# Moving the query and key transposes of an attention plus MoE kernel from TensorE to DMA, from the second batch on

## The chip, the cores and the metric

The kernel runs on one core of one Trainium2 chip. The metric is the device time of one execution in microseconds (us). A ratio is the mean time of one kernel's fast runs over that of the other's fast runs of the same rounds, so it is not quite the ratio of the medians that are quoted; its interval is a 95% one. Differences under 2% count as "the same".

## The reference, cut to what matters

```python
# q, k, v: (4, 8, 768, 64) float32; heads 0, 2, 6 "retrieval", the others "streaming"
scores = q @ k.T / 8            # per batch and head
# retrieval: causal mask; streaming: causal and (first 4 keys, or the last 64)
a = softmax(scores); attn = a @ v
x = attn, heads side by side    # (3072, 512)
p = domain_probs / sum          # (3072, 4)
out = sum over e of p[:, e] * (relu(x @ w1[e]) @ w2[e])   # 4 experts, 512 -> 1024 -> 512
```

## The kernel before

The 3072 rows are cut into eight groups of 384 (two per batch). The MoE (the layer of four experts) of group g and the attention of group g+1 are woven into one stream of work on TensorE (PE): an attention step is put in whenever the attention is behind its share of the MoE time. PE works in program order, so the weaving is fixed when the program is built.

```python
for g in range(G):
    nxt = g + 1
    if nxt < G: att_steps = attention(nxt // NCH, nxt % NCH)
    if g + 2 < G:
        load_qk(...); load_v(...)                 # of group g + 2, GpSimd queue
    begin = 0.55 * UNIT if g == 0 else 0.0        # UNIT: one expert, 10.4 us
    end = 2.6 * UNIT if g == 0 else 0.93 * E * UNIT
    att_ns = 6400.0 if nxt % NCH == 0 else 10200.0
    for ns in moe_group(g):
        spent += ns
        while done < (spent - begin) / (end - begin) * att_ns:
            step = next(att_steps, None)          # ... one attention step
```

A score needs queries and keys with the 64 head dimensions on the partitions, so both are transposed, two heads at a time, by a matmul with the identity, and copied by VectorE (DVE) out of PSUM, the memory that PE writes its results to. `bank()` is one of four PSUM banks that transposes, scores and the first MoE layer take in turn.

```python
def transposes(hp):
    for x, is_k in ((xk, 1), (xq, 0)):
        ps = bank()
        for j in range(3):
            nc.tensor.matmul(out=ps[:, j*P:(j+1)*P], lhsT=x[:, j, 2*hp:2*hp+2, :], rhs=ident, ...)
        # queries: one copy of 128 x 384 to qT[hp]
        # keys: two copies of 64 x 384, each head to its half of a tile whose other half is zero
        ...
```

The softmax here doesn't subtract the row's maximum and nothing guards it: scores larger than these inputs give would overflow.

Of the kernel before, what the change touches and what calls it, by code (L numbers as in the profile page):

```python
# [17 lines left out]
def kernel(  # L18
# [69 lines left out]
    kz = []  # L88
    vR = []
    vS = []  # L90
    for i in range(2):
        kz.append(
            [
                pers.tile([P, NT, P] if not RETR[h] else [P, S], FP16, name=f"kz{i}_{h}")
                for h in range(H)
            ]
        )
        vR.append(pers.tile([P, S // P, len(RH), P], FP16, name=f"vR{i}"))
        vS.append(pers.tile([P, NT, len(SH), P], FP16, name=f"vS{i}"))
# [15 lines left out]
    def v_cols(h):  # L115
        u = h % 2
        return slice(u * D, (u + 1) * D)

# [9 lines left out]
    k16 = {}  # L128
# [7 lines left out]
    def alloc_qk(b, c):  # L136
        q16[b, c] = att.tile([P, 3, H, D], FP16, name="q16", bufs=2)
        k16[b, c] = att.tile([P, 3, H, D], FP16, name="k16", bufs=2)

    def load_qk(b, c):  # L140
        alloc_qk(b, c)
        for x, x16 in ((q, q16[b, c]), (k, k16[b, c])):
            for j in range(3):
                s0 = c * CH + j * P
                gp.dma_start(  # L145
                    out=x16[:, j, :, :],
                    in_=x[b, :, s0 : s0 + P, :].rearrange("h p d -> p h d"),
                )

    def load_v(b, c, heads):  # L150
        for h in heads:
            t = v_tile(b, h)
            if RETR[h]:
                gp.dma_start(  # L154
                    out=t[:, 3 * c : 3 * c + 3, v_cols(h)], in_=rows_of(v, b, h, c)
                )
            else:
                gp.dma_start(  # L158
                    out=t[R0:P, TC * c : TC * (c + 1), v_cols(h)],
                    in_=tiles_of(v, b, h, c),  # L160
                )

    def sink_rows(op, b, h, c):
        t = v_tile(b, h)[:, :, v_cols(h)]
        op(
            out=t[0:NS, TC * c : TC * (c + 1), :],
            in_=t[R0 : R0 + NS, 0:1, :].to_broadcast([NS, TC, D]),
        )
# [30 lines left out]
    def zero_keys(eng, i, h, c):  # L199
        if RETR[h]:  # L200
            fill(eng, kz[i][h][:, c * CH : (c + 1) * CH], 0.0)
        else:
            t = kz[i][h].rearrange("p t x -> p (t x)")
            fill(eng, t[:, c * TC * P : (c + 1) * TC * P], 0.0)
# [38 lines left out]
    for h in range(H):  # L243
        zero_keys(nc.vector, 0, h, 0)
# [47 lines left out]
    load_qk(0, 1)  # L292
# [15 lines left out]
    def attention(b, c):  # L308
        g = b * NCH + c
        i = b % 2  # L310
        qT = {}
# [3 lines left out]
        def transposes(hp):  # L315
            xk, xq, ident = (
                (k32, q32, ident32) if first else (k16[b, c], q16[b, c], ident16)
            )
            qT[hp] = att.tile([P, CH], FP16, name=f"qT{hp}", bufs=2)
            for x, is_k in ((xk, 1), (xq, 0)):  # L320
                ps = bank()
                for j in range(3):
                    o = ps[:, j * P : (j + 1) * P]
                    i_ = x[:, j, 2 * hp : 2 * hp + 2, :]
                    if first:
                        nc.tensor.transpose(o, i_, ident)
                    else:
                        nc.tensor.matmul(out=o, lhsT=i_, rhs=ident, start=True, stop=True)  # L328
                if not is_k:
                    nc.vector.tensor_copy(out=qT[hp], in_=ps[:, 0:CH])  # L330
                    yield 3 * mm_ns(P)
                    continue
                for u in range(2):
                    h = 2 * hp + u
                    r = slice(u * D, (u + 1) * D)
                    if RETR[h]:
                        nc.vector.tensor_copy(  # L337
                            out=kz[i][h][r, c * CH : (c + 1) * CH], in_=ps[r, 0:CH]
                        )
                        continue  # L340
                    nc.vector.tensor_copy(  # L341
                        out=kz[i][h][r, TC * c : TC * (c + 1), R0:P],
                        in_=ps[r, 0:CH].rearrange("r (t x) -> r t x", x=TK),
                    )

                    if b == 0 and c == 0:
                        sink_k[h] = pers.tile([P, NS], FP16, name=f"sk{h}")
                        nc.vector.tensor_copy(out=sink_k[h][r, :], in_=ps[r, 0:NS])
                    if c == 0:
                        nt = TC if b == 0 else NT  # L350
                        nc.vector.tensor_copy(
                            out=kz[i][h][r, 0:nt, 0:NS],
                            in_=ps[r, 0:NS]
                            .rearrange("r (o x) -> r o x", o=1)
                            .to_broadcast([D, nt, NS]),
                        )
                    elif b == 0:
                        nc.scalar.copy(
                            out=kz[i][h][r, TC:NT, 0:NS],
                            in_=sink_k[h][r, :]  # L360
                            .rearrange("r (o x) -> r o x", o=1)
                            .to_broadcast([D, NT - TC, NS]),
                        )
                yield 3 * mm_ns(P)
# [38 lines left out]
        def scores(h):  # L403
            hp = h // 2
            es_of[h] = []
            for cols, parts, masks in score_tiles(h):
                ps = bank()
                ns = 0
                for n, (t, o, q0, nq) in enumerate(parts):
                    lhsT = kz[i][h][:, t * P : (t + 1) * P] if RETR[h] else kz[i][h][:, t, :]  # L410
                    nc.tensor.matmul(  # L411
                        out=ps[:, o : o + nq],
                        lhsT=lhsT,
                        rhs=qT[hp][:, q0 : q0 + nq],
                        start=(n == 0 or not first),
                        stop=not first,
                        skip_group_check=first,
                    )
                    ns += mm_ns(nq)
# [85 lines left out]
        yield from transposes(0)  # L505
        yield from transposes(1)
        if first:

            def sinks(*heads):
                for h in heads:  # L510
                    sink_rows(nc.vector.tensor_copy, b, h, c)
# [13 lines left out]
        else:  # L525
            for h in SH:
                sink_rows(nc.sync.dma_start, b, h, c)
            yield from scores(0)
            for h in range(1, H):
                if h % 2 == 0 and h // 2 + 1 < HP:  # L530
# [78 lines left out]
    for h in range(H):  # L609
        zero_keys(nc.vector, 0, h, 1)  # L610
    for h in range(H):
        zero_keys(gp, 1, h, 0)
        zero_keys(gp, 1, h, 1)
# [17 lines left out]
    for g in range(G):  # L631
# [4 lines left out]
        if g + 2 < G:  # L636
            load_qk((g + 2) // NCH, (g + 2) % NCH)
            load_v((g + 2) // NCH, (g + 2) % NCH, range(H))
# [3 lines left out]
        pos = nxt % NCH  # L642
        att_ns = 6400.0 if pos == 0 else 10200.0
        spent = 0.0
        done = 0.0
        for ns in moe_group(g):
            spent += ns
            while done < (spent - begin) / (end - begin) * att_ns:
# [41 lines left out]
```

## Time and profile before

| | before |
|---|---|
| time, median | 428.46 us |
| span of the profiled run | 426.0 us |
| PE busy | 96% |
| ScalarE (ACT) busy | 59% |
| DVE busy | 47% |
| MoE group 0, with the loading of all weights | 58.1 us |
| groups 1, 3, 5 (attention with 384 keys or fewer inside): "short" | 48.0 us each |
| groups 2, 4, 6 (attention with up to 768 keys inside): "long" | 52.3 us each |
| group 7, no attention inside | 41.5 us |

The group lengths are read from the timeline of PE: a group runs from its first first-layer matmul to that of the next group. They repeat to 0.05 us between groups of a kind; the whole time scatters by 1 to 2 us. The lines themselves stand in the prediction.

### The profile page before, as it was taken

The numbers are of one execution on the slowest core, as the hardware profiler recorded it, in microseconds if no ns is written. First come the engines' busy times: TensorE is split into PE (matmuls) and PEld (weight loads), VectorE is DVE, ScalarE is ACT, GpSimd is POOL, SyncE is SP. The second block draws the span as 40 slices with busy tenths as digits, with TensorE's granted clock in tenths as the row PEclk, the third lists the DMA queues.
The fourth block names the chain that finished last, engine by engine and source line by source line (L and its number), as shares of the span: only waits on it lengthen the run. The fifth ranks groups of instructions, "written<-read, shape, count | busy, mean of one in ns | idle before, by whom it ended". The sixth has DMA issues, their size and how long they took to land.

```text
span 426.0 us, 6784 instructions
## 1 busy us (share of the span) xinstructions
PE 408.4 (96%) x2608; PEld 231.8 (54%) x2608; DVE 198.5 (47%) x433; ACT 251.7 (59%) x544; POOL 101.4 (24%) x155
## 2 busy tenths in 40 slices
PE   6689899999999999999999999999999999999996
PEld 3445554555555555555555555555555555555552
DVE  7657442555525454355545444355544445432222
ACT  5856784356755756556773559646674577653331
POOL 8746915902700045000810009000000000000000
PEclk9989999999999999999999999999999999999999
DMA  9999999932901049100932009120001000020001
GB/s 171 151 184 147 198 209 142 168 24 16 98 33 43 2 31 81 51 26 2 92 21 76 2 0 103 10 76 1 2 0 62 16 0 2 1 75 0 2 0 74
DMA packets 89228, 25.45 MB, mean 60 GB/s; under 512 B 79981, under 2 KB 84077, under 8 KB 89197
## 3 DMA queue, kind: packets, MB, share of 16 engines
q0 software_dynamic: 75552, 17.05, 43.8%
q1 hardware_dynamic: 12044, 7.59, 6.0%
q10 hardware_dynamic: 1600, 0.39, 0.5%
q8 instruction: 20, 0.33, 0.3%
q14 instruction: 12, 0.09, 0.1%
HBM read 35.70 MB, written 6.29 MB: 99 GB/s over the span
## 4 chain that ended last, share of the span: by engine, by line
PE 81%; ACT 8%; DMA 6%; POOL 2%; issue 2%; DVE 1%; POOLq 0%; ACTq 0%
PE pO L572 38%; PE pA L551 32%; PE pV L457 5%; PE pA L411 4%; DMA w2sb<-in_moe_w_dram 3%; ACT hs L564 3%; DMA vR<-in_v_dram 2%; PE pA L328 2%; ACT rc L476 2%; ACT es L429 1%; ACT rc L486 1%; POOL vS L158 1%; POOL vR L154 1%; DVE kz L341 0%; DVE kz L337 0%
## 5 line engine op out<-in xcount | busy, mean ns | idle before, releaser
L551 PE MATMUL pA<-xT,w1sb 128*128 128x384 f16 x1024 | 192.0, 328 | 3.1 <-ACT hs L564 1.7
L572 PE MATMUL pO<-w2sb,hs 128*128 128x512 f16 x768 | 185.1, 379 | 0.0
L564 ACT ACTIVATE hs<-pA 128x384 f16<-128x384 f32 x256 | 121.5, 495 | 89.3 <-PE pA L551 87.7
L551 PEld LDWEIGHTS <-w1sb 128*128 128x128 f16 x1024 | 96.0, 98 | 60.4 <-issue 6.3
L572 PEld LDWEIGHTS <-hs 128*128 128x128 f16 x768 | 72.0, 98 | 69.0 <-ACT hs L564 2.6
L429 ACT ACTIVATE es<-pA 128x256 f16<-128x256 f32 (+3 forms) x152 | 72.1, 486 | 47.0 <-PE pA L411 43.5
L588 DVE SCALAR_TENSOR_TENSOR acc<-pO,p_sb,acc 128x512 f32<-128x512 f32 x72 | 53.9, 749 | 76.9 <-PE pO L572 76.4
L145 POOL DMA_DIRECT2D q<-in_q_dram x21 | 18.6, 895 | 137.1 <-PE pA L411 81.3
L411 PE MATMUL pA<-qT,kz 128*128 128x160 f16 (+5 forms) x300 | 47.6, 244 | 1.6 <-ACT es L429 1.0
L433 DVE TENSOR_TENSOR es<-es,mS 128x384 f16<-128x384 f16 (+1 forms) x70 | 22.2, 317 | 57.7 <-ACT es L429 56.9
L476 ACT ACTIVATE rc<-pV,eps 64x384 f32<-64x384 f32 x60 | 34.6, 576 | 24.2 <-PE pV L457 23.3
L481 DVE TENSOR_TENSOR xT<-pV,rc 64x384 f16<-64x384 f32 x60 | 33.2, 553 | 22.6 <-PE pA L551 11.2
L411 PEld LDWEIGHTS <-kz 128*128 128x128 f16 x300 | 27.3, 98 | 23.0 <-issue 2.3
L486 ACT ACTIVATE rc<-rc 64x384 f32<-64x384 f32 x58 | 30.2, 521 | 1.9
L158 POOL DMA_DIRECT2D vS<-in_v_dram x40 | 28.2, 710 | 9.9 <-DMA w2sb<-in_moe_w_dram 4.3
L433 DVE TENSOR_TENSOR es<-es,mC 128x256 f16<-128x256 f16 (+1 forms) x42 | 10.7, 256 | 36.9 <-ACT es L429 36.9
L584 DVE TENSOR_SCALAR acc<-pO,p_sb 128x512 f32<-128x512 f32 x24 | 18.0, 750 | 17.6 <-PE pO L572 17.5
L341 DVE CAST kz<-pA 64x384 f16<-64x384 f32 x40 | 22.3, 557 | 2.6 <-PE pA L328 1.1
L457 PE MATMUL pV<-es,vR 128*128 128x384 f16 (+2 forms) x120 | 21.7, 278 | 0.8 <-ACT es L429 0.7
L154 POOL DMA_DIRECT2D vR<-in_v_dram x24 | 18.5, 770 | 10.5 <-DMA w2sb<-in_moe_w_dram 5.4
L145 POOL DMA_DIRECT2D k<-in_k_dram x21 | 18.6, 910 | 4.5 <-DMA w2sb<-in_moe_w_dram 4.2
L457 PEld LDWEIGHTS <-vS 128*128 128x128 f16 x180 | 13.9, 98 | 10.4 <-issue 4.7
(60 smaller groups left out, 155.4 us busy)
## 6 DMA issues: line engine op xcount, KB each, us to landing
out_dram<-acc SPq DMA_DIRECT2D x24, 256.0 KB, 2.0
w1sb<-in_moe_w_dram POOLq DMA_DIRECT2D x4, 1024.0 KB, 15.4
w2sb<-in_moe_w_dram POOLq DMA_DIRECT2D x4, 1024.0 KB, 16.4
q<-in_q_dram POOLq DMA_DIRECT2D x21, 128.0 KB, 4.0
k<-in_k_dram POOLq DMA_DIRECT2D x21, 128.0 KB, 5.4
vS<-in_v_dram POOLq DMA_DIRECT2D x40, 48.0 KB, 3.3
vR<-in_v_dram POOLq DMA_DIRECT2D x24, 48.0 KB, 4.0
k<-in_k_dram SPq DMA_DIRECT2D x8, 96.0 KB, 4.0
```

What stands on the lines that cost most here:

```text
L145: gp.dma_start(out=x16[:, j, :, :], in_=x[b, :, s0 : s0 + P, :].rearrange("h p d -> p h d"),)
L411: nc.tensor.matmul(out=ps[:, o : o + nq], lhsT=lhsT, rhs=qT[hp][:, q0 : q0 + nq], start=(n == 0 or not first), stop=not first, skip_group_ ...
L429: nc.scalar.activation(out=es[:, 0:cols], in_=ps[:, 0:cols], func=AF.Exp, scale=SC)
L433: nc.vector.tensor_tensor(out=es[:, o0:o1], in0=es[:, o0:o1], in1=m[:, mo : mo + o1 - o0], op=ALU.mult,)
L457: nc.tensor.matmul(out=ps[:, q0 : q0 + nq], lhsT=v_tile(b, h)[:, t, :], rhs=es[:, o : o + nq], start=(n == 0), stop=(n == len(work) - 1), ...
L476: nc.scalar.activation(out=rc[r, :], in_=ps[o, 0:CH], func=AF.Ln, bias=eps[o, :])
L481: nc.vector.tensor_tensor(out=xT[g][r, hp, :], in0=ps[r, 0:CH], in1=rc[r, :], op=ALU.mult)
L486: nc.scalar.activation(out=rc[r, :], in_=rc[r, :], func=AF.Exp, scale=-1.0)
L551: nc.tensor.matmul(out=pss[ft][:, 0:CH], lhsT=w1sb[:, e * DMP + ct, ft * P : (ft + 1) * P], rhs=xT[g][:, ct, :], start=(ct == 0), stop=(ct ...
L564: nc.scalar.activation(out=hs[:, ft, :], in_=ps[:, 0:CH], func=AF.Relu)
L572: nc.tensor.matmul(out=ps_o, lhsT=hs[:, ft, j * P : (j + 1) * P], rhs=w2sb[:, e * FTP + ft, :], start=(ft == 0), stop=(ft == FTP - 1),)
L588: nc.vector.scalar_tensor_tensor(out=acc[nt], in0=ps_o, scalar=p_ap, in1=acc[nt], op0=ALU.mult, op1=ALU.add,)
```

## The change

The intent: give the 144 transposes of groups 2 to 7 to the DMA engines, so that PE and DVE lose them. Keys are loaded already spread over zeroed 128-column blocks, and five transposing DMAs per group (SBUF to SBUF) turn 41 blocks of 128x128. The pacing of the attention is set anew as well. The core of the diff:

```diff
+    def dma_transposes(b, c):
+        nc.sync.dma_start(out=kSr[c][0:NS, ...], in_=first.to_broadcast(...))   # sink rows
+        alloc_qT(b, c)
+        for j in range(3):
+            nc.sync.dma_start(out=qTs[b, c][:, :, j * P : (j + 1) * P],
+                in_=q16[b, c][:, j, :, :].rearrange("p h d -> p (h d)"), transpose=True)
+        for x, xr in ((kR, kRr), (kS, kSr)):        # 9 and 20 blocks
+            nc.sync.dma_start(out=x[i][:, c, ...], in_=xr[c]..., transpose=True)
...
-        yield from transposes(0)
-        yield from transposes(1)
+        by_dma = b > 0
+        if not by_dma:
+            alloc_qT(b, c)
+            yield from transposes(0)
+            yield from transposes(1)
...
-    for h in range(H):
-        zero_keys(nc.vector, 0, h, 1)
+    zero(nc.vector, kR[0][:, 1, :, :, :])
+    zero(nc.vector, kS[0][:, 1, :, :, :])
...
-            load_qk((g + 2) // NCH, (g + 2) % NCH)
+            load_k(b2, c2)
+            load_q(b2, c2)
...
-        att_ns = 6400.0 if pos == 0 else 10200.0
+        att_ns = 4500.0 if nxt % NCH == 0 else 7700.0
+        if nxt < NCH:
+            att_ns += 8 * 3 * mm_ns(P)
...
+            if to_transpose and spent > 0.5 * E * UNIT:
+                dma_transposes(*divmod(g + 2, NCH))
```

More of the change, by code (lines that the diff above doesn't have):

```diff
@@ L87 @@
     w2sb = pers.tile([P, E * FTP, DM], FP16, name="w2sb")
-    kz = []
+    NR, NSH = len(RH), len(SH)
+    kR = []
+    kS = []
     vR = []
@@ L91 @@
     for i in range(2):
-        kz.append(
-            [
-                pers.tile([P, NT, P] if not RETR[h] else [P, S], FP16, name=f"kz{i}_{h}")
-                for h in range(H)
-            ]
-        )
+        kR.append(pers.tile([P, NCH, 3, NR, P], FP16, name=f"kR{i}"))
+        kS.append(pers.tile([P, NCH, TC, NSH, P], FP16, name=f"kS{i}"))
         vR.append(pers.tile([P, S // P, len(RH), P], FP16, name=f"vR{i}"))
@@ L112, with own, key_tile @@
     p_sb = pers.tile([P, NTILE, E], FP32, name="p_sb")
-    def v_cols(h):
+    kRr = [pers.tile([P, 3, NR, P], FP16, name=f"kRr{c}") for c in range(NCH)]
+    kSr = [pers.tile([P, TC, NSH, P], FP16, name=f"kSr{c}") for c in range(NCH)]
+    def own(h):
         u = h % 2
         return slice(u * D, (u + 1) * D)
+    def key_tile(b, h, t):
+        i = b % 2
+        if RETR[h]:
+            return kR[i][:, t // 3, t % 3, RH.index(h), :]
+        return kS[i][:, t // TC, t % TC, SH.index(h), :]
     def v_tile(b, h):
@@ L127 @@
     q16 = {}
-    k16 = {}
     def rows_of(x, b, h, c):
@@ L134, in tiles_of, with load_by_rows, load_q, load_k @@
         return x[b, h, c * CH : (c + 1) * CH, :].rearrange("(t r) d -> r t d", r=TK)
-    def alloc_qk(b, c):
-        q16[b, c] = att.tile([P, 3, H, D], FP16, name="q16", bufs=2)
-        k16[b, c] = att.tile([P, 3, H, D], FP16, name="k16", bufs=2)
-    def load_qk(b, c):
-        alloc_qk(b, c)
-        for x, x16 in ((q, q16[b, c]), (k, k16[b, c])):
-            for j in range(3):
-                s0 = c * CH + j * P
+    def load_by_rows(x, x16, b, c):
+        for j in range(3):
+            s0 = c * CH + j * P
+            gp.dma_start(
+                out=x16[:, j, :, :],
+                in_=x[b, :, s0 : s0 + P, :].rearrange("h p d -> p h d"),
+            )
+    def load_q(b, c):
+        q16[b, c] = att.tile([P, 3, H, D], FP16, name="q16", bufs=2)
+        load_by_rows(q, q16[b, c], b, c)
+    def load_k(b, c):
+        for h in range(H):
+            if RETR[h]:
                 gp.dma_start(
-                    out=x16[:, j, :, :],
-                    in_=x[b, :, s0 : s0 + P, :].rearrange("h p d -> p h d"),
-                )
+                    out=kRr[c][:, :, RH.index(h), own(h)], in_=rows_of(k, b, h, c)
+                )
+            else:
+                gp.dma_start(
+                    out=kSr[c][R0:P, :, SH.index(h), own(h)], in_=tiles_of(k, b, h, c)
+                )
+    qTs = {}
+    def alloc_qT(b, c):
+        qTs[b, c] = att.tile([P, HP, CH], FP16, name="qT", bufs=2)
+    def dma_transposes(b, c):
+        i = b % 2
+        first = kSr[0][R0 : R0 + NS, 0:1, :, :].rearrange("p t s x -> p t (s x)")
+        nc.sync.dma_start(
+            out=kSr[c][0:NS, :, :, :].rearrange("p t s x -> p t (s x)"),
+            in_=first.to_broadcast([NS, TC, NSH * P]),
+        )
+        alloc_qT(b, c)
+        for j in range(3):
+            nc.sync.dma_start(
+                out=qTs[b, c][:, :, j * P : (j + 1) * P],
+                in_=q16[b, c][:, j, :, :].rearrange("p h d -> p (h d)"),
+                transpose=True,
+            )
+        for x, xr in ((kR, kRr), (kS, kSr)):
+            nc.sync.dma_start(
+                out=x[i][:, c, :, :, :].rearrange("p t s x -> p (t s) x"),
+                in_=xr[c].rearrange("p t s x -> p (t s x)"),
+                transpose=True,
+            )
     def load_v(b, c, heads):
@@ L154, in load_v @@
                 gp.dma_start(
-                    out=t[:, 3 * c : 3 * c + 3, v_cols(h)], in_=rows_of(v, b, h, c)
+                    out=t[:, 3 * c : 3 * c + 3, own(h)], in_=rows_of(v, b, h, c)
                 )
@@ L158, in load_v, with sink_row, sink_rows @@
                 gp.dma_start(
-                    out=t[R0:P, TC * c : TC * (c + 1), v_cols(h)],
+                    out=t[R0:P, TC * c : TC * (c + 1), own(h)],
                     in_=tiles_of(v, b, h, c),
                 )
-    def sink_rows(op, b, h, c):
-        t = v_tile(b, h)[:, :, v_cols(h)]
-        op(
+    def sink_row(b, h, c):
+        t = v_tile(b, h)[:, :, own(h)]
+        nc.vector.tensor_copy(
             out=t[0:NS, TC * c : TC * (c + 1), :],
             in_=t[R0 : R0 + NS, 0:1, :].to_broadcast([NS, TC, D]),
+        )
+    def sink_rows(b, c):
+        x = vS[b % 2].rearrange("p t s x -> p t (s x)")
+        nc.sync.dma_start(
+            out=x[0:NS, TC * c : TC * (c + 1), :],
+            in_=x[R0 : R0 + NS, 0:1, :].to_broadcast([NS, TC, NSH * P]),
         )
@@ L197, in fill, with zero @@
             eng.memset(ap, value)
-    def zero_keys(eng, i, h, c):
-        if RETR[h]:
-            fill(eng, kz[i][h][:, c * CH : (c + 1) * CH], 0.0)
-        else:
-            t = kz[i][h].rearrange("p t x -> p (t x)")
-            fill(eng, t[:, c * TC * P : (c + 1) * TC * P], 0.0)
+    def zero(eng, t):
+        fill(eng, t.rearrange("p t s x -> p (t s x)"), 0.0)
     def one_values(eng, i, c):
@@ L242 @@
     load_v(0, 0, [0, 1, 2, 3])
-    for h in range(H):
-        zero_keys(nc.vector, 0, h, 0)
+    zero(nc.vector, kR[0][:, 0, :, :, :])
+    zero(nc.vector, kS[0][:, 0, :, :, :])
     nc.vector.tensor_copy(out=ident16, in_=ident32)
@@ L291 @@
     load_w2(0)
-    load_qk(0, 1)
+    load_q(0, 1)
+    k16 = att.tile([P, 3, H, D], FP16, name="k16", bufs=1)
+    load_by_rows(k, k16, 0, 1)
     load_w1(1, 0, F)
@@ L310, in attention @@
         i = b % 2
-        qT = {}
         first = g == 0
@@ L316, in transposes @@
             xk, xq, ident = (
-                (k32, q32, ident32) if first else (k16[b, c], q16[b, c], ident16)
+                (k32, q32, ident32) if first else (k16, q16[b, c], ident16)
             )
-            qT[hp] = att.tile([P, CH], FP16, name=f"qT{hp}", bufs=2)
             for x, is_k in ((xk, 1), (xq, 0)):
@@ L329, in transposes @@
                 if not is_k:
-                    nc.vector.tensor_copy(out=qT[hp], in_=ps[:, 0:CH])
+                    nc.vector.tensor_copy(out=qTs[b, c][:, hp, :], in_=ps[:, 0:CH])
                     yield 3 * mm_ns(P)
@@ L337, in transposes @@
                         nc.vector.tensor_copy(
-                            out=kz[i][h][r, c * CH : (c + 1) * CH], in_=ps[r, 0:CH]
+                            out=kR[i][r, c, :, RH.index(h), :],
+                            in_=ps[r, 0:CH].rearrange("r (t x) -> r t x", x=P),
                         )
                         continue
+                    n = SH.index(h)
                     nc.vector.tensor_copy(
-                        out=kz[i][h][r, TC * c : TC * (c + 1), R0:P],
+                        out=kS[i][r, c, :, n, R0:P],
                         in_=ps[r, 0:CH].rearrange("r (t x) -> r t x", x=TK),
                     )
-                    if b == 0 and c == 0:
+                    sinks = kS[i][r, c, :, n, 0:NS]
+                    if c == 0:
                         sink_k[h] = pers.tile([P, NS], FP16, name=f"sk{h}")
                         nc.vector.tensor_copy(out=sink_k[h][r, :], in_=ps[r, 0:NS])
-                    if c == 0:
-                        nt = TC if b == 0 else NT
-                        nc.vector.tensor_copy(
-                            out=kz[i][h][r, 0:nt, 0:NS],
-                            in_=ps[r, 0:NS]
-                            .rearrange("r (o x) -> r o x", o=1)
-                            .to_broadcast([D, nt, NS]),
-                        )
-                    elif b == 0:
-                        nc.scalar.copy(
-                            out=kz[i][h][r, TC:NT, 0:NS],
-                            in_=sink_k[h][r, :]
-                            .rearrange("r (o x) -> r o x", o=1)
-                            .to_broadcast([D, NT - TC, NS]),
-                        )
+                        src, op = ps[r, 0:NS], nc.vector.tensor_copy
+                    else:
+                        src, op = sink_k[h][r, :], nc.scalar.copy
+                    src = src.rearrange("r (o x) -> r o x", o=1)
+                    op(out=sinks, in_=src.to_broadcast([D, TC, NS]))
                 yield 3 * mm_ns(P)
@@ L409, in scores @@
                 for n, (t, o, q0, nq) in enumerate(parts):
-                    lhsT = kz[i][h][:, t * P : (t + 1) * P] if RETR[h] else kz[i][h][:, t, :]
                     nc.tensor.matmul(
                         out=ps[:, o : o + nq],
-                        lhsT=lhsT,
-                        rhs=qT[hp][:, q0 : q0 + nq],
+                        lhsT=key_tile(b, h, t),
+                        rhs=qTs[b, c][:, hp, q0 : q0 + nq],
                         start=(n == 0 or not first),
@@ L510, in sinks @@
                 for h in heads:
-                    sink_rows(nc.vector.tensor_copy, b, h, c)
+                    sink_row(b, h, c)
             yield from scores(0)
@@ L525, in attention @@
         else:
-            for h in SH:
-                sink_rows(nc.sync.dma_start, b, h, c)
+            sink_rows(b, c)
             yield from scores(0)
             for h in range(1, H):
-                if h % 2 == 0 and h // 2 + 1 < HP:
+                if not by_dma and h % 2 == 0 and h // 2 + 1 < HP:
                     yield from transposes(h // 2 + 1)
@@ L608 @@
     to_mask(mS[:, 3, :], bS[:, 2, :])
-    for h in range(H):
-        zero_keys(nc.vector, 0, h, 1)
-    for h in range(H):
-        zero_keys(gp, 1, h, 0)
-        zero_keys(gp, 1, h, 1)
+    zero(nc.vector, kR[0][:, 1, :, :, :])
+    zero(nc.vector, kS[0][:, 1, :, :, :])
+    for c in range(NCH):
+        zero(gp, kRr[c])
+        zero(gp, kSr[c])
     one_values(gp, 1, 0)
@@ L636 @@
         if g + 2 < G:
-            load_qk((g + 2) // NCH, (g + 2) % NCH)
-            load_v((g + 2) // NCH, (g + 2) % NCH, range(H))
+            b2, c2 = divmod(g + 2, NCH)
+            load_k(b2, c2)
+            load_q(b2, c2)
+            load_v(b2, c2, range(H))
         begin = 0.55 * UNIT if g == 0 else 0.0
         end = 2.6 * UNIT if g == 0 else 0.93 * E * UNIT
-        pos = nxt % NCH
-        att_ns = 6400.0 if pos == 0 else 10200.0
+        att_ns = 4500.0 if nxt % NCH == 0 else 7700.0
+        if nxt < NCH:
+            att_ns += 8 * 3 * mm_ns(P)
         spent = 0.0
         done = 0.0
+        to_transpose = g + 2 < G
         for ns in moe_group(g):
             spent += ns
+            if to_transpose and spent > 0.5 * E * UNIT:
+                dma_transposes(*divmod(g + 2, NCH))
+                to_transpose = False
             while done < (spent - begin) / (end - begin) * att_ns:
```

## The prediction

> **What bounds the kernel now.** I read the busy shares on the page first, then the table of stretches cut at the ends of the eight MoE groups (a group is 384 rows; the attention of group g+1 is woven into the MoE of group g), then the timeline of TensorE.
>
> ```profile
> PE 408.4 (96%) x2608; PEld 231.8 (54%) x2608; DVE 198.5 (47%) x433; ACT 251.7 (59%) x544; POOL 101.4 (24%) x155
> ```
>
> That is the busy time of each engine over the span of 426.0 us. From the table of stretches, groups 1 and 2 of the MoE:
>
> ```profile
> 80.50:128.50 48.00, 47.72 (x310) 27.39 (x308) 24.10 (x54) 29.17 (x65) 15.46 (x21) 1.00 0.68 62
> 128.50:180.80 52.30, 51.54 (x342) 29.52 (x340) 24.11 (x48) 32.69 (x71) 10.96 (x14) 1.00 0.40 39
> ```
>
> Each row has the stretch, its length, then busy us of PE, weight loads, DVE, ACT and POOL, then the granted clock. PE is busy for 47.72 of 48.00 and 51.54 of 52.30 us; no other engine passes 63%. So the order of work on PE is the time, from about 21 us on. Groups 3 and 5 repeat the 48.0, groups 4 and 6 the 52.2 to 52.3.
>
> A busy PE is not a PE at its peak, so I split a group by starts rather than durations:
>
> ```profile
> 153.36 0.33 PE L328 MATMUL pA<-ident,k 128*128 128x128 f16 x3
> 153.53 1.03 PE L572 MATMUL pO<-w2sb,hs 128*128 128x512 f16 x4
> 154.39 0.33 PE L328 MATMUL pA<-ident,q 128*128 128x128 f16 x3
> 154.56 0.33 PE L411 MATMUL pA<-qT,kz 128*128 128x64 f16 x3
> ```
>
> Three transposes hold PE from 153.36 to 153.53, and again from 154.39 to 154.56: 0.17 us, 56 ns each, not the 219 ns that the group's row gives as a duration. Four matmuls of 512 columns take 0.86 us. In the last group, which has no attention, a whole expert takes 10.38 us (its second-layer blocks start at 385.52 and 395.90), four of them 41.5 us. Attention of an even group has 5184 columns of scores and as many of values, of an odd one 8960 and 8960; at the spacing seen (columns over 2.4 GHz plus 2.5 ns) that is 4.5 and 7.6 us. 24 transposes per group are 24 x 0.056 = 1.34 us. So the work is 41.5 + 4.5 + 1.3 = 47.3 of 48.0 us, and 41.5 + 7.6 + 1.3 = 50.5 of 52.3 us: lost are 0.7 and 1.8 us per group, more than the recorded idle time, since a modelled end hides up to 0.17 us of each gap.
>
> **What the skill says.** "TensorE: Matmul & The Clock Gate", section "Wait — 56ns, not 53.3ns?", gives columns over 2.4 GHz plus about 2.5 ns from start to start, 55.6 ns at 128 columns; the 56 ns above agree. "VectorE: DVE Perf Modes", section "The three transpose paths", gives 1309 ns for one 128x128 block by DMA against 390 on TensorE. "DMA: Bandwidth & Descriptors", section "Latency and other measured facts", gives a transposing DMA an effective 261 GB/s in one kernel. The same page, section "Issuing engines are not separate DMA queues", says all queues share the same 16 engines and interleave. The trace of before has no transposing DMA, so the two DMA durations are untested here; that sharing matters is likely, since the DMA row of the page reads 9 tenths for the first 85 us.
>
> **The change part by part.**
>
> Removed from PE: in six groups (2 to 7) 24 transposes each, 144 x 56 ns = 8.06 us. PE is the bound in all these stretches, so it comes off the end one for one.
>
> Removed from DVE: per group 4 copies of qT at 556 ns, 8 of keys at about 550, and the sink copies, some 7 us, about 42 us in six groups. DVE is half idle, so this gives nothing by itself. But each transpose also took one of the four PSUM banks that scores and layer 1 rotate through, eight takes in about 60 per group, and waits of PE and its weight loads for "DVE kz" come up in the list of waits (2.1 and 0.7 us in all). The pacing changes too: the attention was given 10200 or 6400 "ns" to be spread over, and with 9.0 and 5.8 of real work it was finished after about 82 to 84% of the group; now 7700 and 4500 fit the real 7.6 and 4.5, and it is spread over 92%. ScalarE (Exp beside ReLU) is what PE stalls on in dense places, so of the 6 x about 1.2 = 7.3 us lost I let a third go: 2.2 us, the least certain gain. The order of the built program shows the last scaling of attention still two DVE additions ahead of the group's end, about 2 us, so the later finish should not delay the next group's layer 1.
>
> Added: per group three transposing DMAs for q (12 blocks), one for 9 blocks of retrieval keys, one for 20 blocks of streaming keys, 41 blocks or 1.34 MB, all on the sync queue, plus one small DMA for the sink rows; key loads go from 3 to 8 DMAs of the same bytes. How long do 41 blocks take? At the skill's 261 GB/s 5.1 us. From the trace: the plain hardware queue moved 12044 packets in 6.0% of 16 engines' span, 6.0% x 16 x 426 / 12044 = 34 ns a packet; with 256-byte rows a block is 128 packets, 41 x 128 x 34 / 16 = 11 us. At 1309 ns a block, one after another, 54 us. I take 5 to 11 us.
>
> From group 3 on that is hidden. The sync queue can start the transposes for g+2 once the outputs of g-1 are issued and the loads are in, so early in the MoE of g, and PE needs them a group later, some 45 us. The DMA engines are nearly idle there (share 0.03 from 129 to 155 us).
>
> Group 2 is different. Its loads queue behind the expert weights:
>
> ```profile
> 57.83 0.88 POOL L145 DMA_DIRECT2D k<-in_k_dram  x1 [4.22 <-DMA w2sb<-in_moe_w_dram]
> 62.74 0.74 POOL L154 DMA_DIRECT2D vR<-in_v_dram  x1 [4.03 <-DMA w1sb<-in_moe_w_dram]
> 67.82 0.73 POOL L158 DMA_DIRECT2D vS<-in_v_dram  x1 [4.34 <-DMA w2sb<-in_moe_w_dram]
> ```
>
> POOL keeps eight DMAs open and waits for the eighth before; the last weights land at 67.8. In before, six q and k loads were issued by 58.7. Now eight key loads come first, so the eighth key load waits until 67.8, and the three q loads after it until their own slots free. From 67.5 to 87 us the loads of groups 2 and 3 (18432 rows of 64) keep the DMA engines full, about 1.06 ns a row, so the 6144 rows of k and q of group 2 are in at about 67.5 + 6.5 = 74 to 75. Only then can the transposes go, with values of group 2 and all loads of group 3 (about 12 us of DMA time) beside them. If each side gets half, q (12 of 41 blocks) lands at about 78 to 81, retrieval keys at 80 to 85, streaming keys at 85 to 91. PE reaches the first score of group 2 about 0.5 us into the MoE of group 1, at 81, and the first streaming head some 3 us later, at 84. PE issues in order, so it stands still for 1 to 7 us; I take 4.
>
> Sum: 428.6 - 8.1 - 2.2 + 4 = 422.3; the start-up (memsets merged, the same area) gives nothing. I say 422.
>
> **The rivals.** (1) No stall at group 2: the transposes run at the skill's rate and the load order costs nothing. For: the weights are in at 67.8 and 13 us are left. Against: the DMA row is full until 87. It would give 418 to 419, and with more of the lost time won back 416.5. (2) Transposing DMA is slow, near 1.3 us a block in a row: 54 us exceed a group of 48 us, PE waits in every group, and the time is 440 or more. For: the only figure for a single block. Against: that figure carries one DMA's fixed latency, and the change moves 9 to 20 blocks per transfer. I give it 6%. (3) The freed PE time turns into waits for ScalarE, because the same Exp and ReLU fall into a shorter group: then the 0.7 and 1.8 us grow and the gain is 4 to 6 us. For: ACT is the engine named at most short stalls of PE. Against: ACT is busy 61 to 63% of a group and would be at 64%, and the attention is spread wider.
>
> **Range and chances.** The removed 8.1 us are firm: alone 420.6, 1.9%, just inside the 2% line (420.07). Stall recovery (0 to 4) and the wait at group 2 (0 to 10, with a tail) set the rest. Range 416.5 to 428.5. Faster by over 2% needs the wait at group 2 to stay below about 1.7 us at my recovery: 0.36. Within 2%: 0.54. Slower: 0.10, from rival 2 and a very long wait at group 2.
>
> **What would show it.** Groups 3 to 6 should be 46 to 46.7 us (even attention) and 50 to 51 us (odd), with 24 fewer matmuls each, and about 7 us less DVE time. A wait of PE for a DMA into qT, kR or kS should stand once, at 81 to 85 us, of some us; none later. The transposes of a later group should land within 5 to 15 us of their first issue. I am wrong in kind if PE waits for DMA in later groups, if group lengths shrink by less than 1.3 us, or if the transposes' landing takes tens of us.

## The result, and the profile after

The changed kernel takes 423.05 us (422.07 to 424.63, four runs) against 428.46: ratio 0.9876, interval 0.9844 to 0.9907, the same by the 2% rule and 5.4 us faster.

The engines' busy times after, from the page's first part (the span is 422.7 us, and this profiled run is the slowest of the four):

```profile
PE 401.9 (95%) x2464; PEld 225.8 (53%) x2464; DVE 159.1 (38%) x334; ACT 251.7 (60%) x544; POOL 120.0 (28%) x173
```

PE has 144 matmuls fewer and DVE 99 instructions and 39 us less; ScalarE is as before. The table of stretches, cut at the groups (length, then busy us of PE, weight loads, DVE, ACT and POOL, which is GpSimd; granted clock, DMA share, GB/s; the share adds up packets that overlap in time and can pass 1), groups 0 to 3:

```profile
21.46:81.11 59.65, 55.94 (x341) 31.02 (x342) 27.98 (x62) 35.19 (x79) 34.93 (x51) 0.94 1.41 169
81.11:134.12 53.01, 48.26 (x283) 26.44 (x282) 17.53 (x36) 29.69 (x64) 39.43 (x54) 0.97 1.52 129
134.12:184.07 49.95, 49.54 (x317) 28.34 (x316) 17.70 (x36) 32.37 (x70) 0.75 (x1) 1.00 0.21 45
184.07:230.59 46.52, 46.24 (x283) 25.98 (x282) 17.53 (x36) 29.34 (x64) 27.36 (x37) 1.00 1.09 97
```

Groups 2 and 3 fell from 52.30 to 49.95 and from 47.96 to 46.52 us; groups 4 to 6 repeat these. Group 1 did not fall: it rose from 48.0 to 53.0. Over the run that is 3 x 2.35 + 2 x 1.44 = 9.9 us won in groups 2 to 6, 5.0 lost in group 1, and 1.5 lost in group 0, which leaves the 3.3 us between the two profiled spans.

What happens in group 1 stands in the timeline of PE (start, length, instructions, idle time before them and its releaser):

```profile
81.11 0.81 PE L591 MATMUL pA<-xT,w1sb 128*128 128x384 f16 x4
83.63 0.39 PE L449 MATMUL pA<-qT,kR 128*128 128x128 f16 x2 [1.71 <-DMA kR<-kRr]
83.86 1.46 PE L591 MATMUL pA<-xT,w1sb 128*128 128x384 f16 x8
85.16 0.27 PE L449 MATMUL pA<-qT,kR 128*128 128x256 f16 x1
85.27 1.46 PE L591 MATMUL pA<-xT,w1sb 128*128 128x384 f16 x8
89.49 0.31 PE L449 MATMUL pA<-qT,kS 128*128 128x160 f16 x2 [2.76 <-DMA kS<-kSr]
89.64 2.10 PE L591 MATMUL pA<-xT,w1sb 128*128 128x384 f16 x8
```

The first score of group 2 comes one chunk of layer 1 into the group, and PE stands for the retrieval keys (kR) and then for the streaming keys (kS). These are the only two DMA waits of PE into qT, kR or kS in the whole run. Then something else: the last eight matmuls take 2.10 us where the eight before took 1.46. The table of stretches shows why, in its clock column (before the DMA share):

```profile
85.00:89.50 4.50, 1.74 (x12) 0.89 (x10) 0.23 (x1) 1.94 (x5) 3.60 (x5) 1.00 1.80 198
90.30:93.73 3.43, 3.43 (x13) 1.73 (x12) 0.33 (x1) 2.12 (x5) 2.07 (x4) 0.50 1.78 245
```

After the idle time the throttle grants half the clock for 3.4 us, which costs another 1.7 us of work.

The sync queue's own timeline, for group 2 and for group 4, shows when the transposes were issued:

```profile
71.89 0.64 SPq L176 DMA_DIRECT2D kSr<-kSr  x1
73.63 4.82 SPq L182 DMA_TRANSPOSE qT<-q  x3
78.55 1.51 SPq L188 DMA_TRANSPOSE kR<-kRr  x1
80.15 4.73 SPq L188 DMA_TRANSPOSE kS<-kSr  x1
...
137.19 3.83 SPq L182 DMA_TRANSPOSE qT<-q  x3
141.14 1.28 SPq L188 DMA_TRANSPOSE kR<-kRr  x1
142.52 3.05 SPq L188 DMA_TRANSPOSE kS<-kSr  x1
```

In the packet records the 5248 packets of 256 bytes of one set (41 x 128) run from 138.37 to 147.04 us in group 4, 8.7 us with the engines nearly free, and from 75.55 to 87.17 in group 2, 11.6 us beside the loads. PE was let go later still: 1.1 us after the last packet of group 2's retrieval keys (82.48) and 2.3 us after the last of its streaming keys (87.17), whose completions stand at 88.8 to 89.5 in the trace. Group 4's keys are there 37 us before they are needed; group 2's could not start earlier, because its loads came last, as the timeline of POOL shows:

```profile
64.23 0.75 POOL L160 DMA_DIRECT2D kRr<-in_k_dram  x1 [4.24 <-DMA w1sb<-in_moe_w_dram]
69.33 0.72 POOL L164 DMA_DIRECT2D kSr<-in_k_dram  x1 [4.34 <-DMA w2sb<-in_moe_w_dram]
70.03 2.66 POOL L147 DMA_DIRECT2D q<-in_q_dram  x3
```

The eighth key load waited for the last weights, and the queries went after it. The order on the sync queue adds to this: the last load of retrieval keys was issued at 64.23 us, but their transpose stands behind those of the queries and was issued at 78.55. Whether another order would have shortened the wait was not tested.

### The profile page after: what moved, and what is told of

Read it like the earlier page. It is cut to its first block, busy times and chain, and to the rows that moved or that the text cites. A ratio compares the mean times of both kernels' runs of the same rounds, so it can differ in the third digit from the quotient of the medians.

```text
span 422.7 us, 6420 instructions
## 1 busy us (share of the span) xinstructions
PE 401.9 (95%) x2464; PEld 225.8 (53%) x2464; DVE 159.1 (38%) x334; ACT 251.7 (60%) x544; POOL 120.0 (28%) x173
## 4 chain that ended last, share of the span: by engine, by line
PE 74%; DMA 16%; POOL 5%; ACT 3%; issue 1%; DVE 0%; SPq 0%; POOLq 0%
PE pO L612 34%; PE pA L591 31%; DMA w2sb<-in_moe_w_dram 7%; DMA w1sb<-in_moe_w_dram 6%; PE pV L495 4%; PE pA L449 4%; DMA kS<-kSr 2%; ACT hs L604 2%; POOL vS L202 1%; DMA vS<-in_v_dram 1%; POOL vR L198 1%; ACT rc L514 1%; POOL q L147 1%; ACT es L467 0%; POOL w2sb L228 0%
## 5 line engine op out<-in xcount | busy, mean ns | idle before, releaser
L612 PE MATMUL pO<-w2sb,hs 128*128 128x512 f16 x768 | 182.1, 381 | 0.0
L591 PEld LDWEIGHTS <-w1sb 128*128 128x128 f16 x1024 | 98.2, 99 | 60.8 <-issue 5.1
L612 PEld LDWEIGHTS <-hs 128*128 128x128 f16 x768 | 73.4, 98 | 73.7 <-issue 1.4
L164 POOL DMA_DIRECT2D kSr<-in_k_dram x30 | 20.9, 700 | 54.3 <-DMA kSr<-kSr 43.8
L449 PE MATMUL pA<-qT,kS 128*128 128x160 f16 (+2 forms) x180 | 23.5, 222 | 4.9 <-DMA kS<-kSr 2.8
L449 PE MATMUL pA<-qT,kR 128*128 128x384 f16 (+2 forms) x120 | 25.1, 278 | 2.7 <-DMA kR<-kRr 1.7
L449 PEld LDWEIGHTS <-kS 128*128 128x128 f16 x180 | 15.7, 98 | 16.9 <-issue 3.6
L160 POOL DMA_DIRECT2D kRr<-in_k_dram x18 | 13.5, 752 | 25.2 <-DMA kR<-kRr 20.2
L495 PEld LDWEIGHTS <-vS 128*128 128x128 f16 x180 | 13.8, 98 | 10.3 <-issue 3.9
```

What stands on the lines that cost most here:

```text
L449: nc.tensor.matmul(out=ps[:, o : o + nq], lhsT=key_tile(b, h, t), rhs=qTs[b, c][:, hp, q0 : q0 + nq], start=(n == 0 or not first), stop=no ...
L495: nc.tensor.matmul(out=ps[:, q0 : q0 + nq], lhsT=v_tile(b, h)[:, t, :], rhs=es[:, o : o + nq], start=(n == 0), stop=(n == len(work) - 1), ...
L591: nc.tensor.matmul(out=pss[ft][:, 0:CH], lhsT=w1sb[:, e * DMP + ct, ft * P : (ft + 1) * P], rhs=xT[g][:, ct, :], start=(ct == 0), stop=(ct ...
L612: nc.tensor.matmul(out=ps_o, lhsT=hs[:, ft, j * P : (j + 1) * P], rhs=w2sb[:, e * FTP + ft, :], start=(ft == 0), stop=(ft == FTP - 1),)
```

## The experiments

Three calls of four kernels each. The kernel of before had a median of 427.94, 427.96 and 428.25 us in them. Group lengths are from each run's profile.

| run | time, us | ratio to before | group 0 | 1 | long (2, 4, 6) | short (3, 5) |
|---|---|---|---|---|---|---|
| before | 428.46 | 1 | 58.1 | 47.96 | 52.30 | 47.96 |
| the change | 423.05 | 0.9876 | 59.6 | 53.0 | 49.95 | 46.52 |
| e0_again | 423.95 | 0.9904 | 57.5 | 53.5 | 49.95 | 46.52 |
| e1_late_start | 417.16 | 0.9748 | 57.0 | 46.37 | 49.95 | 46.52 |
| e2_old_pacing | 427.02 | 0.9983 | 57.8 | 54.0 | 50.29 | 46.52 |
| e3_before_new_pacing | 427.47 | 0.9989 | 59.5 | 47.99 | 51.95 | 47.96 |
| e4_pe_dummies | 424.52 | 0.9914 | 58.3 | 48.3 | 50.65 | 47.88 |
| e5_double | 416.62 | 0.9735 | 58.3 | 46.37 | 49.95 | 46.52 |
| e6_one_block | 505.19 | 1.1801 | 57.6 | 81.1 | 58.5 to 65.2 | 55.9, 56.3 |
| e7_split_memsets | 422.84 | 0.9888 | 58.3 | 51.7 | 49.95 | 46.52 |
| e8_late_split | 417.37 | 0.9752 | 58.8 | 46.37 | 49.95 | 46.53 |
| e11_late_again | 417.57 | 0.9755 | 57.6 | 46.37 | 49.95 | 46.52 |
| e9_dummies_copies | 428.65 | 1.0011 | 59.3 | 48.5 | 51.95 | 47.88 |
| e10_dve_only | 418.70 | 0.9783 | 58.8 | 48.2 | 49.95 | 46.54 |

### The change once more

No edit.

> The changed kernel once more, unedited, as the base for the others of this call and to see which parts of its trace repeat. Expected 421 to 424 us. In the first profile the MoE of group 0 was 59.65 us against 58.11 in before, with a second stretch of half clock at 32 us. If this is the change (theory: memsets merged into long ones on DVE held POOL up and its loads by 0.5 us), group 0 is again 59 us or more. If it is scatter of the DMA (rival), it falls back to about 58.

Measured 423.95 us. Group 0 is 57.5 us, shorter than in before, so the 1.5 us that the first profile lost there are scatter; over all runs group 0 lies between 57.0 and 59.6 us with no order by kernel. Group 1 is 53.5 us again, with waits of 2.3 and 2.7 us and half a clock from 89.0 to 92.4 us. That loss belongs to the change.

### Starting the attention of group 2 later

```diff
-        begin = 0.55 * UNIT if g == 0 else 0.0
+        begin = {0: 0.55, 1: 1.0}.get(g, 0.0) * UNIT
```

> The attention of group 2 starts one expert (10.4 us) into the MoE of group 1 instead of at its begin, so PE reaches the first scores at about 91.5 us, after the streaming keys, which PE got at 89.5. Theory (PE stood for the transposes of group 2 and then lost clock): group 1 falls from 53.0 us to 46.5 to 47.0, the half clock at 90 us is gone, the total falls by 6 to 6.5 us, to about 416.5 to 417. Rival (the wait only moves, to values, or denser attention makes new stalls on ScalarE): a fall of less than 3 us.

Measured 417.16 us, ratio 0.9748 (0.9735 to 0.9762): 6.8 us (1.6%) less than the unedited kernel, and faster than before by the 2% rule. The first scores in the timeline of PE:

```profile
90.53 0.81 PE L591 MATMUL pA<-xT,w1sb 128*128 128x384 f16 x4
91.18 0.38 PE L449 MATMUL pA<-qT,kR 128*128 128x128 f16 x2
91.40 1.47 PE L591 MATMUL pA<-xT,w1sb 128*128 128x384 f16 x8
92.70 0.27 PE L449 MATMUL pA<-qT,kR 128*128 128x256 f16 x1
92.81 0.81 PE L591 MATMUL pA<-xT,w1sb 128*128 128x384 f16 x4
93.46 0.30 PE L449 MATMUL pA<-qT,kS 128*128 128x160 f16 x2
```

No idle time stands before any of them, and the group's row has the full clock:

```profile
80.15:126.52 46.37, 46.14 (x283) 25.95 (x282) 17.57 (x36) 29.19 (x64) 39.45 (x54) 1.00 1.65 146
```

So in the change group 1 lost 53.02 - 46.37 = 6.65 us: 4.47 of recorded waits, 1.7 of clock, and 0.5 that is not taken apart (part of it lies in the waits, which the modelled ends of matmuls shorten in the record). The theory holds; the rival, that the wait would only move, falls. The repeat, e11_late_again, gave 417.57 us and the same 46.37:

> The late start unedited, as the base of this call: 416.5 to 417.5 us again, group 1 46.4 us.

### The pacing, in both kernels

In the changed kernel the attention is spread over the share of a group that it had in before; in the kernel of before, over the new share.

```diff
 # changed kernel
-        att_ns = 4500.0 if nxt % NCH == 0 else 7700.0
+        att_ns = 4920.0 if nxt % NCH == 0 else 8680.0
         if nxt < NCH:
-            att_ns += 8 * 3 * mm_ns(P)
+            att_ns = 10200.0
 # kernel of before
-        att_ns = 6400.0 if pos == 0 else 10200.0
+        att_ns = 5840.0 if pos == 0 else 9040.0
```

> The changed kernel with the attention spread over the same share of a group as in before (84 and 82% instead of 92%). Theory (the wider spread brought the 1.0 us that even groups won beyond the transposes): groups 2, 4 and 6 become 0.5 to 1.0 us longer each, total 1.5 to 3 us more than the unedited one. Rival (it was the eight bank takes and DVE copies that are gone): no more than 0.5 us in all.

> The kernel of before with the attention spread over 92% of a group, as in the changed one, transposes on PE as they were. Theory (pacing): 1.5 to 3 us faster than before, 425.5 to 427. Rival (banks): within 0.5 us of before.

The long groups became 0.34 us longer in the one (50.29 for 49.95) and 0.35 shorter in the other (51.95 for 52.30); the short ones did not move. Pacing is worth 0.35 us in each long group, about 1 us in all, a third to two thirds of what the theory said. In the time of the second kernel this does not show: 427.47 against 427.94 us, with an interval (0.9977 to 1.0001) that includes 1. The time of the first kernel, 3 us over the unedited kernel, misleads: only 1.0 us of it is in the long groups. The rest is a longer wait of group 1 (4.4 us for kS), group 0, and 1.1 us after the last matmul.

### Needless transposes back on PE

24 transposes of q per group in groups 2 to 7, into banks that nobody reads; the result stays right.

```diff
+        def dummies(hp):
+            for _ in range(2):
+                ps = bank()
+                for j in range(3):
+                    nc.tensor.matmul(out=ps[:, ...], lhsT=q16[b, c][...], rhs=ident16, ...)
+                yield 3 * mm_ns(P)
```

> The changed kernel with 24 needless transposes of q put back on PE in each of groups 2 to 7, written to PSUM banks that nobody reads, so without the DVE copies. Theory (a transpose costs PE its 56 ns one for one, because PE is the bound): groups 3 and 5 grow from 46.5 to 47.9 us, the total by 8 us, less what the later stop at group 2 hides (dummies for q run while the keys are awaited, up to 0.7 us): 430 to 431.5. Rival (PE had slack that took the transposes in): less than 4 us more.

Measured 424.52 us, far less than expected, and the expectation erred twice. First, the four dummy steps stand ahead of the first score and are paced like the others, so PE came to it some us later and waited 0.2 us for a DMA instead of 4.5; this run must be held against the late start (417.2), not against the unedited kernel. Second, the 1.34 us of PE time cost 1.36 us in a short group but only 0.70 in a long one:

```profile
128.85:179.50 50.65, 50.65 (x341) 29.65 (x340) 17.64 (x36) 32.91 (x70) 9.08 (x12) 1.00 0.45 61
179.50:227.38 47.88, 47.65 (x307) 27.30 (x306) 17.26 (x36) 29.56 (x64) 19.00 (x26) 1.00 0.73 78
```

In the long groups about half of the transposes ran in time in which PE would have waited, and the traces name the wait. Each long group of the change has one recorded stop of PE in its middle, at a score that waits for ScalarE's ReLU (`hs`) to empty a bank; the first is

```profile
163.32 0.33 PE L449 MATMUL pA<-qT,kS 128*128 128x64 f16 x3 [0.35 <-ACT hs L604]
```

From start to start it is 0.52 us. With the dummies PE has no recorded stop in a long group.

### The same with copies, and copies alone

```diff
 # e9: the dummies, with the old copies out of their banks
+                for r in (slice(0, D), slice(D, P)) if is_k else (slice(0, P),):
+                    nc.vector.tensor_copy(out=junk[r, :], in_=ps[r, 0:CH])
 # e10: no matmuls and no banks, twelve copies per group from SBUF
+                    nc.vector.tensor_copy(out=junk, in_=ident32...to_broadcast([P, 4, P]))
```

> The needless transposes of the earlier run, now with the DVE copies out of their banks as in before (one of 128x384 or two of 64x384 each). Groups 2, 4, 6 were 52.30 us in before, 51.95 there with the wider spread, 50.65 with needless transposes but no copies, 49.95 with neither. Theory (the copies, and the banks they hold, make the rest of the gain): 51.9 us in those groups again, about 427 to 428 in all. Rival (the gain comes from the new key layout or from the loads): they stay near 50.65.

> Twelve copies on DVE per group at the places of the old ones, from SBUF to SBUF, without matmuls and without PSUM banks. Theory (a bank is held until its copy is done, and that makes PE wait): groups 2, 4, 6 stay at 49.95 to 50.2 us. Rival (it is DVE's time: masks and scalings come later behind the copies): they grow towards 51.3 us, as copies with banks added 1.3.

With the copies the long groups are back at 51.95 us, to the hundredth what the kernel of before has with the new pacing; the time is 428.65 us, and the whole gain is gone. The row of a long group in this run, and then the one of the run with copies alone:

```profile
129.01:180.97 51.96, 50.95 (x342) 29.70 (x341) 24.23 (x48) 33.15 (x70) 9.09 (x12) 1.00 0.44 59
```

```profile
128.24:178.19 49.95, 49.83 (x318) 28.33 (x316) 21.66 (x48) 32.89 (x70) 0.76 (x1) 1.00 0.21 45
```

Copies alone add 4 us of DVE time to the 17.7 of the changed kernel and nothing to the group. So it is not DVE's time as such, though these copies took 418 ns each against 558 for those out of PSUM, so that a small share of it is not excluded. (The time of this run, 418.70 us, is above the late start: PE waited 1.5 us for kS in group 1 again, and by the 2% rule it is unclear.)

The same copies as readers of PSUM banks add 1.30 us to a long group (50.65 to 51.95) and none to a short one. The trace shows where. Laid beside the long group of the dummies alone, start by start, PE falls behind twice, by 0.67 us each, and nowhere else. Both times it stops at a layer 1 chunk that needs a bank, right after the second of two transposes:

```profile
144.93 0.81 PE L608 MATMUL pA<-xT,w1sb 128*128 128x384 f16 x4 [0.51 <-ACT hs L621]
158.50 0.81 PE L608 MATMUL pA<-xT,w1sb 128*128 128x384 f16 x4 [0.51 <-ACT hs L621]
```

Two of the four banks hold transposes that are being copied, and the next one in turn is still being read by the ReLU of the chunk before last. With the dummies alone, whose banks nobody reads, the same chunk started at once, before that ReLU had begun. The kernel of before with the new pacing has the same two stops (0.51 and 0.50 us, at 144.31 and 157.89). So what costs the 1.30 us is that the transposes hold banks; the wait itself is named after ScalarE, and it is not a copy that PE waits for. Nor is it a mask that comes late because DVE stands behind a copy: neither stop is at a matmul that uses masked scores.

### Every transposing DMA twice

```diff
+        again = 2 if b > 1 else 1
-        for j in range(3):
+        for j in list(range(3)) * again:
-        for x, xr in ((kR, kRr), (kS, kSr)):
+        for x, xr in ((kR, kRr), (kS, kSr)) * again:
```

> The late start of the attention of group 2 kept, and in groups 4 to 7 every transposing DMA issued twice, to the same place. One set took 8.7 us alone in the trace (first to last 256-byte packet), two take about 17, of some 45 us that are there. Theory (hidden from group 3 on): within 0.5 us of the late start alone, 416.5 to 417. Rival (the DMA engines or the sync queue are near their limit, outputs or loads are held up): 2 us or more slower.

Measured 416.62 us with every group length as with the late start. The doubled set of group 4 took 18.5 us of packets (130.37 to 148.82) and cost nothing. So a second set of transposes would still have been in time; the experiment does not say how much more would.

### One block per transfer

```diff
-            nc.sync.dma_start(out=x[i][:, c, ...], in_=xr[c]..., transpose=True)
+            for m in range(r.shape[1] // P):
+                nc.sync.dma_start(out=o[:, m : m + 1, :], in_=r[:, m * P : (m + 1) * P], transpose=True)
 # and the queries likewise, with the late start kept
```

> Late start kept; one 128x128 block per transposing DMA, 41 DMAs per group instead of 5. In the changed kernel the sync queue took 1.27 us to issue 4 blocks, 1.3 for 9, 3.05 for 20, so about 1.0 us fixed and 0.1 a block. Theory (fixed cost per DMA): 41 x 1.1 = 45 us per group, the sync queue is busy a whole group, PE waits in most groups, 430 us or more. Rival (the cost goes with blocks, issues overlap): 10 to 20 us per group, hidden from group 3 on, and only group 2 waits some us more than with the late start: 417 to 422.

Measured 505.19 us, with long and short groups of 56 to 65 us. The sync queue's timeline in one group:

```profile
130.15 16.07 SPq L183 DMA_TRANSPOSE qT<-q  x12
146.27 11.44 SPq L194 DMA_TRANSPOSE kR<-kRr  x9
157.75 26.34 SPq L194 DMA_TRANSPOSE kS<-kSr  x20
```

Each issue takes 1.3 us, whichever tile: 41 x 1.31 = 54 us of a queue that works in order, longer than a group, and PE's recorded waits for DMA from the first score of group 2 on sum to 66 us. In the change 9 blocks in one transfer took the same 1.28 us. That many blocks go in one transfer is what makes the change work.

### Short memsets at the start

```diff
-        fill(eng, t.rearrange("p t s x -> p (t s x)"), 0.0)
+        t = t.rearrange("p t s x -> p (t s x)")
+        for a in range(0, t.shape[1], 512):
+            fill(eng, t[:, a : min(a + 512, t.shape[1])], 0.0)
```

> The changed kernel with its long memsets of key tiles (1280 floats a partition, 1.24 us) cut into pieces of 512 halves, so that none is longer than 0.3 us, as in before. Theory (a long DVE memset held up POOL at 5 to 6 us, where two affine selects took 1.13 us instead of 0.54, and so the loads): these selects take 0.54 us again, the weights are issued 0.5 us earlier, group 0 ends earlier and the total falls by 0.5 to 1.5 us. Rival (group 0 is scatter of the DMA): no difference in time beyond 0.5 us.

> Late start of the attention of group 2 together with the memsets cut small: the candidate for the best kernel. In the split run POOL's two affine selects were back to 0.54 us and the first weights were issued at 11.23 instead of 11.81 us. Theory (half a microsecond earlier weights move the whole loading phase): 0.5 to 1 us faster than the late start alone of this call, about 416.3. Rival (group 0 scatters between 57 and 60 us anyway and hides it): equal within 0.5 us.

The half microsecond is real. POOL's two selects, and the issue of the first weights, with the long memsets (first fence, the change once more) and with short ones (second):

```profile
4.88 1.13 POOL L310 TENSOR_SCALAR_AFFINE_SELECT bC<-bC 128x128 f16<-128x128 f16 x2
...
11.81 0.76 POOL L222 DMA_DIRECT2D w1sb<-in_moe_w_dram  x1
```

```profile
4.89 0.54 POOL L312 TENSOR_SCALAR_AFFINE_SELECT bC<-bC 128x128 f16<-128x128 f16 x2
...
11.23 0.76 POOL L222 DMA_DIRECT2D w1sb<-in_moe_w_dram  x1
```

But no time comes of it: with the late start 417.37 against 417.57 us, intervals overlapping almost wholly. Group 0 scatters more than that. Which DVE instruction held POOL up, the memset or the cast right after it, is open; the edit moved both.

## Why the prediction was right

It said 422, range 416.5 to 428.5, most likely within 2%; 423.05 us was measured. Step by step:

- **8.06 us off PE, "one for one".** Put back alone, the transposes cost 1.36 us in a short group for 1.34 predicted, but 0.70 in a long one; over three of each, 6.2 us. In the long groups PE also stops for banks, and there a transpose less is not simply its length less.
- **2.2 us of lost time regained.** Mis-sized, and the weights were wrong: the wider spread gave 0.35 per long group (1.05 us), but the banks that transposes no longer hold gave 1.30 (3.9 us). "This gives nothing by itself", said of DVE's time, was right; the bank takes named beside it were worth more than the pacing. How the gain divides between this point and the first depends on the order in which parts are put back. Counted by PE's stops of over 0.1 us (from start to start, less the columns' own time), a long group lost 1.57 us in before, 1.34 with dummies and copies, 0.74 in the change and nothing with dummies alone; by that count the whole 1.34 us came off and 0.8 us of stops with it. Either way, groups 1 to 6 without any wait, as in the late start, are 11.5 us shorter than before, where 10.3 was predicted.
- **A wait of 1 to 7 us, taken as 4, once, at 81 to 85 us.** The place was right in the main (it came in two parts, for kR to 83.6 and for kS from 86.7 to 89.5), and so was the cause, the key load that stood until the last weights landed. The loss was 6.65 us, because the half clock after it (1.7 us) was not thought of. Keys at 83.6 and 89.5 lie inside the 80 to 85 and 85 to 91 that were worked out.
- **5 to 11 us for 41 blocks, hidden from group 3 on.** 8.7 us measured, 11.6 with traffic beside it; doubled it cost nothing.
- **The start-up gives nothing.** In time, yes.

More was gained than predicted (11.5 for 10.3 us) and more was lost (6.65 for 4). The two errors partly cancel, so that 422 lies within about 1 us of the measured time is in part luck. Two slips of the working change nothing: by its own formula the attention of an odd group is 7.7 us, with which its sum of 50.5 is right, and of the waits for kz the 2.1 us are those of the weight loads and the 0.7 those of PE.

The sum with the measured terms, for a run whose group 0 is as long as before's: -6.2 - 3.9 - 1.05 - 0.4 (not taken apart) + 6.65 = -4.9 us, beside 5.4 between the medians; group 0's scatter covers the difference. Of the rivals, (1) is what the late start turned the kernel into, (2) is what happens with one block per transfer, and (3), ScalarE taking up the freed time, did not come as such: the groups shrank by 1.44 and 2.35 us, although the one stop that is left in a long group does wait for ScalarE.

## What to carry to other kernels

Work moved off the bound engine must also arrive in time at the first place that uses it: here one late arrival at the start took back 6.65 of 11.5 us, and moving that first use 10 us down the program, one line, made the kernel 2.5% faster than before instead of 1.0%. Price a removed instruction by what it holds as well as by its length: half of the gain of a long group came from PSUM banks that the transposes no longer held. And a transposing DMA has a price per transfer (1.3 us to issue 1, 4 or 9 blocks, 3 us for 20), so give it many blocks.

## What the Trainium skill lacked or had wrong

- "VectorE: DVE Perf Modes", section "The three transpose paths": its 1309 ns for a 128x128 block by DMA is close to the issue time of a one-block transfer here (1.31 us each over 41 issues), but it does not grow in step with the blocks, as the table may suggest: 9 blocks in one took 1.28 us to issue, 20 took 3.05.
- "DMA: Bandwidth & Descriptors", section "Latency and other measured facts": its 261 GB/s, and 350 to 400 for the contiguous case, were not reached over a whole set. 41 blocks are 1.34 MB; in 8.7 us with the engines nearly free that is 155 GB/s (1.5 us of it lie between issues, with no packet; the 29 key blocks after them ran at 201), and beside loads, in 11.6 us, 116. Only one stretch of 1.5 us in the doubled run passed 261, with 287 GB/s.
- "TensorE: Matmul & The Clock Gate", section "Why this matters for your kernels", warns of PE gaps over about 3 us. Here a recorded gap of 2.76 us brought half the clock for 3.4 us, and in the run with short memsets one of 2.15 us, right before the clock fell, did so too, while one of 2.27 us in the change once more (to 82.94) did not. In the two that did, PE had been busy for 0.83 and 1.26 of the 3.41 us before the fall.
- No page prices PSUM banks that transposes hold: eight banks per group, held for their copies, cost 1.30 us in the long groups and nothing measurable in the short ones.
